# Dummy products among the first weight folds, one key-value step later, nine fill products less, and w_in loaded by halves of its rows

## The chip, the cores and the metric

The kernel runs on one core of a Trainium2 chip. The metric is the device time of one execution in microseconds; three runs of the kernel before took 252.22, 252.37 and 252.92 us, the median is 252.37. Five engines work side by side, each on its own list of instructions in order: TensorE (PE, with the loading of its weights as PEld), VectorE (DVE), ScalarE (ACT), GpSimd (POOL) and SyncE (SP), which issues DMAs. Semaphores order them among each other.

## The reference

A block of two parts over one sequence of 2048 rows of 448 columns. `mod` gives a shift, a scale and a gate for each part from a vector `c`.

```
mod = silu(c) @ w_mod                       # sa, ca, ga, sb, cb, gb: 448 each
h = layernorm(x) * (1 + ca) + sa
qkv = h @ wqkv                              # 16 heads of 28
phi_k = softmax(k w_phi), softmax(-k w_phi) # the same for q
kv, z = sum over rows of phi_k x v, of phi_k
x = x + ga * ((phi_q kv) / (phi_q z + 1e-6)) @ wo
h = layernorm(x) * (1 + cb) + sb
z = gelu(h @ w_in)                          # 1792 columns: z1 and z2
g = w_sp @ layernorm(z2) + b_sp             # w_sp is 2048 x 2048
x = x + gb * ((z1 * g) @ w_out)
```

## The kernel before

The rows are cut into 16 tiles of 128. The order of all work is written out by hand: the string `ORDER` is a list of words, each one step of the program, and every engine does its share of the steps in that order. A word such as `kM:10@B1` names the step (`kM`), its arguments (tile 10) and the PSUM bank that it writes (`@B1`); `/V`, `/S`, `/G` name the engine. There are five banks or pairs of banks, `A0` to `A2` and `B0`, `B1`, and a new tile in a bank waits until the old one is read, or, if nobody read it, until it is written.

The steps that the change and the prediction touch, with their lines:

- `du` (L725): dummy products of 128 x 256 zeros into a bank, read by nobody. 28 of them stand at the program's start.
- `ct` (L736) turns the row `c` into columns in bank `B0`; `ce:1` to `ce:4` (L743 to L749) make silu(c) of it, `f_scol`, the last step on VectorE.
- `csA`, `ccA` (L760) multiply w_mod's first two sections by `f_scol`: 16 products of one column each. `esA` puts the shift into `f_Ga` (L767), `ecA` the scale into `f_ca` (L764).
- `FTk`, `ETk`, `FSk`, `PFk`, `EPk` fold w_phi into the key weights: transposes on TensorE (L809) and copies (L813, L815), one-column products with the shift (L826), products with a block matrix (L836), and copies scaled by `f_ca` into `f_Wk` (L787 on VectorE, L783 on ScalarE). `FTq`, `ETq` and so on do it for the query. `SHv` (L774) is the shift of the value weights. `X` (L867) transposes a tile of x.
- `kM`, `vM` (L877, L885) are the key and value products of a tile, `kE`, `kF` (L880) the exponentials, `kS`, `kR`, `kP` (L891, L895, L898) the sums, their reciprocals and the normalised features `f_phik`, and `kA` (L908) the key-value step: it adds phi_k x v of one tile to `kvacc`.
- `nM` (L960) is the numerator's product, `dm` (L965) fill products of 32 zero columns into an unused part of its bank, `SHw` (L779) the shift of w_in's columns, 448 at a time, over all 448 rows in four blocks; `SCw` (L783, L785, L787) scales w_in in place. `wM` and `wN` (L996, and L994 with x added on TensorE) are the products with wo.
- `ld:win0`, `ld:win1` load w_in on ScalarE's DMA queue.

After these come the products with w_in (L1040, L1069), the large product with w_sp (L1115, L1136) and the one with w_out (L1150).

Of the kernel before, what the change touches and what calls it, by code (L numbers as in the profile page):

```python
# [15 lines left out]
P = 128  # L16
# [5 lines left out]
FH = 896  # L22
# [459 lines left out]
ORDER = """du:2@A1 ld:wk/S ld:x1/Y l1s:1 l1e:1,2/V l1r:1,2 tbl du:3@A2 ld:c/S du:3@A0 m1/G ld:x0/Y ld:wsa/Y m2a/V du:3@B1 du:14@A1 m4 ld:phi/Y du:3@B0 l1s:0 ct@B0  # L482
l1e:0,1/G l1a:1/V FTk:0@A0 ce:1 m3 ld:x2/Y X:1@A1 XE:1/V ce:2 ce:3 ce:4 ETk:0/S FTk:1@A2 ETk:1/S l1s:3 csA@B1 l1r:0,1 ld:wca/Y esA m2b/V l1a:0/G X:0@A2
bd/G FSk@A0 l1s:2 FCk/V ccA@A1 l1e:2,4/G PFk:1@B1 ecA EPk:1/V l1r:2,4 l1a:2/G XE:0/S ld:wv/Y PFk:3@A2 ld:wq/Y PFk:0@B0 EPk:0/S PFk:2@A0 ld:x5/S SHv@A1
SCv:0/S EPk:2/V EPk:3/V kM:0@B0 l1a:3/V SCv:2/V FTq:0@B1 ld:x3/Y SCv:1/S ETq:0/V kE:0 FTq:1@A1 ld:x4/Y ld:wmgb/S ETq:1/S X:2@A2 XE:2/V kF:0 kM:1@A0 l1s:4
FSq@B1 l1s:5 X:3@A1 kF:1 PFq:1@A2 l1s:6 kE:1 kM:2@B0 l1s:7 SCv:3/G FCq/S EPq:1/S XE:3/S vM:1@A0 vC:1 kS:1 vM:0@B1 ld:wo/S PFq:3@A2 kF:2 PFq:2@A0 vM:3@A1
kE:2 vM:2@B0 EPq:3/S PFq:0@A2 scb l1s:9 vC:0 ld:wmga/S vC:3 EPq:0/S kM:3@B1 EPq:2/S gr:1@A1 l1s:11 l1s:13 vC:2 qM:1@A0 kE:3 kF:3 qE:1 kS:0 l1e:4,8/G l1r:4,8
kR:0 gr:0@B1 ge:0 ge:1 qF:1 qM:0@A2 l1s:8 kR:1 qE:0 l1a:6/G l1a:4/G l1a:5/G l1s:10 T1:4,6 l1a:7/G T1:6,8 kM:4@B0 kM:5@B1 l1s:12 kP:0/G l1s:15 qF:0 kS:2
kR:2 kE:4 kS:3 l1s:14 qM:2@A1 kA:0@A0 kP:1/G kR:3 kF:4 kP:3/V kE:5 qF:2 kA:1@A0 l1e:8,12/G kP:2/V W:0,4 l1e:12,16/V kM:7@B0 kF:5 kF:7 kS:4 kE:7 kS:5 kA:2@A0
kR:5 kP:5/V l1r:8,12 l1a:8/G l1a:9/G l1a:11/G kA:3@A0 kM:6@A2 vM:5@B0 vM:4@B1 wos:0/G wos:3/V l1a:10/G T1:8,10 kR:4 kS:7 qE:2 l1r:12,16 vC:5 kP:4/V kF:6  # L490
kE:6 kS:6 kR:6 kP:6/V T1:10,12 vC:4 kM:9@A1 vM:6@B0 l1a:13/G kR:7 ld:wcb/Y ld:wsb/S l1a:14/G l1a:12/G T1:12,14 kM:8@A2 kE:9 kF:8 l1a:15/G kE:8 kP:7/G vC:6
kS:8 kA:4@A0 kM:10@B1 kR:8 kF:9 kP:8/G kS:9 kE:10 kA:5@A0 T1:14,16 vM:8@A2 kF:10 vM:9@A1 kR:9 kP:9/G vC:8 vC:9 kM:11@B0 vM:7@A2 vC:7 kS:10 kM:12@A1 kE:11
kF:11 kE:12 kR:10 kA:6@A0 kA:7@A0 kS:11 vM:10@A2 kM:14@B0 kP:10/V kF:12 kR:11 vC:10 ld:wout/Y kS:12 kF:14 vM:11@A1 vC:11 ld:win0/S kM:13@B1 vM:12@A2 kR:12
kE:14 kA:8@A0 kP:11/G W:0,0 kF:13 kM:15@B0 kS:14 kE:13 vC:12 kE:15 kA:9@A0 kS:13 kR:13 kP:12/G kF:15 ld:win1/S kS:15 kP:13/V vM:14@B1 vM:15@A2 vM:13@B0
kR:14 vC:13 kA:10@A0 kA:11@A0 kR:15 kP:14/V kA:12@A0 vC:14 kA:13@A0 kA:14@A0 kP:15/V vC:15 kA:15@A0 KV:0/V KV:1/V qM:3@A2 KZ:0 KZ:1 nM:0@A1 wos:1/V qE:3
nX:0 nM:1@A0 nX:1 qF:3 csB@B0 esB nC:1 ccB@B1 SHw:2@B0 qM:4@A2 nC:0 nS:0 nT:0 nA:0/G qM:5@A1 wos:2/G nT:1 T2:0,1 qE:4 nA:1/V qF:4 T2:1,2 W:0,1 nM:2@A0
nX:2 ecB SCw:0,2/V nC:2 nM:3@A2 nX:3 SHw:1@B1 wN:0@B0 qE:5 SCw:0,1/S nC:3 nS:1 nT:2 SHw:3@B1 nM:4@A0 nT:3 qF:5 nM:5@A1 SCw:0,3/S wN:1@B1 nX:4 wR:0/S nA:2/G
nX:5 wQ:0/S nA:3/V wR:1/S T2:2,4 wQ:1/S W:0,6 W:1,0 nC:4 nC:5 nS:2 dm:9,3 SHw:0@B0 SCw:0,0/S nT:4 qM:6@A2 qF:6 wts:6/V nT:5 nA:4/V nA:5/V nM:7@A0 nM:6@A1
wN:3@B1 nX:7 T2:4,6 SCw:1,0/G nX:6 qE:6 wN:2@B0 wR:3/S SCw:3,1/G nC:7 wR:2/S nC:6 nS:3 SCw:2,1/V nT:7 nT:6 nA:6/V qM:7@A2 W:0,3 l2R:0,2/G wQ:3/S l2r:0,2
l2a:1/G wQ:2/S qE:7 nM:9@A0 nM:8@A1 SCw:1,1/V l2a:0/G nX:8 nC:8 wN:4@B1 wM:5@B0 nX:9 nC:9 T3:0,1 qF:7 zM:0@A2 nA:7/G l2R:2,4/G SCw:3,0/V wR:4/S gt nS:4  # L500
nT:9 T2:6,8 nT:8 nM:10@A0 wM:6@B1 zG:0 nM:11@A1 T3:1,2 nX:10 nX:11 wR:5/V l2r:2,4 l2a:3/G l2a:2/G T3:2,4 wR:6/V W:1,3 wQ:4/V zM:1@A2 nC:11 nC:10 nA:9/G
SCw:2,0/S wQ:5/S wM:7@B1 zG:1 l2R:4,6/G l2r:4,6 nA:8/V T2:8,10 yM:0,0@B0 yG:0,0 W:0,7 nM:13@A2 nX:13 nS:5 zQ:0/S nT:10 wR:7/V wQ:7/S nT:11 nA:11/V zQ:1/V
zM:2@A0 zG:2 zR:0,2/V wQ:6/S zM:3@A1 nM:12@A0 wts:0/V wM:8@B0 l2a:4/G nX:12 zG:3 nC:13 l2a:5/G T3:4,6 l2R:6,8/G nA:10/V l2r:6,8 wM:9@B1 zM:4@A1 zG:4 nC:12
nS:6 nT:13 nM:15@A2 wR:8/V T2:10,12 nT:12 wQ:8/S l2a:6/G l2a:7/G wR:9/V zW:0,2 yM:0,1@B0 nM:14@A1 nX:15 T3:6,8 W:2,3 nC:15 wts:3/G zM:5@A0 nX:14 yG:0,1
wQ:9/S nC:14 nS:7 zQ:3/S yM:0,4@B1 yG:0,4 wts:1/G nA:12/V nT:14 wN:11@B0 nA:13/V wR:11/S nT:15 yM:1,3@B1 yG:1,3 wN:10@A1 zQ:2/V W:0,5 zN:1/G yM:1,1@B1
zM:6@A2 nA:14/G zN:0/G zG:5 yG:1,1 wR:10/S nA:15/V W:2,5 wQ:11/S T2:12,14 yM:0,5@B1 T2:14,16 W:2,4 zR:2,4/V yG:0,5 wM:12@B0 wQ:10/V l2R:10,12/V l2R:8,10/V
l2r:10,12 l2a:10/V zW:2,4 zQ:4/S wM:13@A0 wR:13/V yM:1,0@B1 wR:12/V wQ:12/V W:1,1 zQ:5/S zN:2/G yG:1,0 zG:6 yM:1,5@A1 l2r:8,10 wQ:13/V l2R:12,14/G yG:1,5
wts:4/V zM:7@A0 l2a:8/V zG:7 wM:14@B0 wR:14/V wM:15@B1 W:2,2 zQ:6/S l2r:12,14 W:2,7 l2a:9/G T3:8,10 zQ:7/S yM:1,4@A1 yG:1,4 wR:15/V wQ:15/S l2a:11/V yM:0,2@A2
ld:bsp/Y T3:10,12 W:1,7 l2a:12/V zR:4,6/G zR:6,8/V zW:4,6 zN:4/G yM:0,3@B1 yM:1,6@B0 l2a:13/V yG:0,2 zN:3/V yM:1,2@A0 yG:1,6 zM:9@A2 guard@A1 yG:1,2 zG:9
zN:5/V zM:8@A0 zW:6,8 zM:10@A1 zG:8 wQ:14/V l2R:14,16/G l2r:14,16 yG:0,3 yM:2,1@B0 zG:10 zN:7/G zM:11@A0 yM:2,6@A1 zN:6/V l2a:14/V T3:12,14 zQ:8/V zQ:9/S  # L510
zG:11 yG:2,6 W:1,4 zM:13@A2 zR:8,10/G zW:8,10 wts:5/V yM:2,2@A0 zM:12@A1 zQ:11/S zQ:10/V yG:2,2 zN:8/G W:2,0 yM:2,5@B1 zG:13 l2a:15/V T3:14,16 W:1,2 yM:2,4@A2
zR:10,12/G zW:10,12 yG:2,1 zG:12 W:0,2 zQ:12/S zQ:13/V yM:3,6@A0 yG:2,4 yG:3,6 zM:14@A1 yG:2,5 W:1,5 zN:9/V zM:15@A2 yM:3,3@A0 zG:14 yG:3,3 zN:11/V zN:10/V
zG:15 zQ:14/V yM:3,0@B1 zQ:15/S yM:3,1@A1 yM:3,2@A2 yG:3,2 wts:2/V yM:2,0@A0 W:2,1 yG:3,1 yM:3,5@B0 yG:3,5 yM:0,6@A2 W:1,6 sS:0,1,0,8/V sS:0,2,0,8/V yG:2,0
yM:3,4@A1 yM:2,3@A0 zR:12,14/V zR:14,16/G zW:14,16 tT:1,1/V tT:1,0/V zN:14/V zW:12,14 zN:15/V zN:13/G yG:2,3 yG:0,6 yG:3,0 zN:12/V tT:3,0/V tT:2,0/V gM:1@B0
sS:0,3,0,8/V yG:3,4 gal tT:2,1/V tT:1,2/V P:0,1,1 tT:2,2/V P:0,0,1 P:0,0,7 W:3,2 P:0,0,6 sS:0,4,0,8/V W:2,6 d:0,0,1 W:3,5 P:0,1,6 d:0,1,1 d:0,1,3 d:0,0,2
tT:3,2/V tT:4,0/G gM:0@B1 d:0,0,3 P:0,0,2 tT:4,2/G P:0,0,5 gG:1 gG:0 d:0,0,4 x:0,0,4/G P:0,1,5 d:0,0,5 W:3,4 d:0,0,7 P:0,2,1 W:3,1 P:0,0,3 P:0,0,4 d:0,0,6
d:0,1,2 x:0,0,6/V d:0,0,8 d:0,1,5 x:0,0,8/V tT:3,1/V P:0,1,2 W:3,0 d:0,1,4 P:0,2,6 P:0,1,3 x:0,0,7/V d:0,2,1 d:0,2,3 d:0,2,2 x:0,1,4/G P:0,2,7 P:1,0,1
# [740 lines left out]
```

## Time and profile before

| | |
|---|---|
| Median of three runs | 252.37 us |
| The profiled execution | 252.36 us |
| Its span, first to last instruction | 250.5 us |
| TensorE busy | 243.3 us (97%), 1517 products |
| VectorE busy | 185.4 us (74%) |
| ScalarE, GpSimd busy | 104.2 us (42%), 125.2 us (50%) |
| Mean granted TensorE clock | 0.992 |
| Chain of waits by engine | PE 77%, DVE 12%, POOL 4%, DMA 3% |

All times below count from the span's start. The chain of waits is followed back from the last instruction: at each step to what released it, or to the instruction before it on its engine. A row of the timeline gives the start, the time from there to the end of the last of a merged group, the engine, the line, the operation, out<-in and the count; in brackets stands idle time ahead of it and what ended it. Products are pipelined, so the length of one is more than the distance from one to the next. The granted clock is 1.00 at full speed.

### The profile page before, as it was taken

The page shows a single profiled execution, that of the slowest core. Times are in us where ns is not written, and L with a number is a line of the kernel's source. Part 1 is how long each engine was busy: PE and PEld are TensorE (multiplying, and loading weights), DVE is VectorE, ACT ScalarE, POOL GpSimd, SP SyncE. Part 2 cuts the span into 40 slices and gives each one's busy share as a digit, 9 for nine tenths or more (in the row PEclk, how much of TensorE's full clock was granted, in tenths as well). Part 3 has the DMA queues.
Part 4 walks back from the last instruction along what each step waited for, and adds up shares of the span by engine and source line. Part 5 has one row for each costly group of instructions (what it writes and reads, how often), then busy time and mean ns, then how long its engine had stood idle before and what let it go on. Part 6 is the DMA issues. An engine that isn't in the chain of part 4 may idle for free.

```text
span 250.5 us, 4157 instructions
## 1 busy us (share of the span) xinstructions
PE 243.3 (97%) x1517; PEld 127.0 (51%) x1517; DVE 185.4 (74%) x371; ACT 104.2 (42%) x220; POOL 125.2 (50%) x166
## 2 busy tenths in 40 slices
PE   7999999999999999999999999999999999999993
PEld 5765565666656554444444444444444444444451
DVE  5869999987799999885359799496876435644552
ACT  2488986836988966986777300000000000000000
POOL 3718996713298685586816764110119511024430
PEclk9889999999999999999999999999999999999999
DMA  7986559870587969789790981000001000101022
GB/s 176 267 245 154 104 111 257 178 190 1 94 155 139 153 125 177 131 145 219 136 171 1 179 160 41 3 0 0 0 3 38 0 0 3 55 0 37 18 79 82
DMA packets 68655, 25.22 MB, mean 101 GB/s; under 512 B 58129, under 2 KB 68498, under 8 KB 68626
## 3 DMA queue, kind: packets, MB, share of 16 engines
q1 hardware_dynamic: 64848, 20.78, 42.1%
q10 hardware_dynamic: 3778, 4.09, 6.2%
q8 instruction: 14, 0.23, 0.4%
q14 instruction: 15, 0.12, 0.2%
HBM read 8.87 MB, written 1.84 MB: 43 GB/s over the span
## 4 chain that ended last, share of the span: by engine, by line
PE 77%; DVE 12%; POOL 4%; DMA 3%; issue 1%; ACT 1%; DVEq 0%; POOLq 0%
PE g_ps L1115 29%; PE o_ps L1150 8%; PE z_ps L1069 7%; PE z_ps L1040 7%; PE g_ps L1136 6%; PE x_ps L996 3%; DVE f_ksum L891 3%; PE v_ps L885 3%; DVE f_st L843 3%; PE k_ps L877 2%; PE q_ps L932 2%; PE kvacc L908 2%; PE num L960 2%; PE warm_ps L725 2%; DMA f_hT<-f_xpad 2%; DMA f_ar<-f_ar 1%
## 5 line engine op out<-in xcount | busy, mean ns | idle before, releaser
L1124 DVE TENSOR_TENSOR f_zb<-g_ps,f_zb 128x512 f32<-128x512 f32 (+1 forms) x31 | 20.3, 668 | 18.5 <-PE g_ps L1115 18.1
L1115 PEld LDWEIGHTS <-f_z2n 128*128 128x128 bf16 x192 | 18.8, 98 | 22.5
L1131 POOL TENSOR_TENSOR f_z1T<-f_zb,f_z1T 128x512 bf16<-128x512 f32 (+1 forms) x11 | 12.0, 1102 | 35.6 <-DVE f_zb L1124 35.6
L1040 PE MATMUL z_ps<-f_ar,f_hT 112*128 112x448 bf16 (+1 forms) x128 | 26.7, 352 | 0.5 <-DMA f_hT<-f_xpad 0.5
L1069 PE MATMUL z_ps<-f_hT,f_ar 113*128 113x512 bf16 (+1 forms) x112 | 26.4, 378 | 0.1
L1150 PE MATMUL o_ps<-f_wout,f_z1T 128*128 128x448 bf16 x112 | 22.5, 352 | 0.0
L1115 PE MATMUL g_ps<-f_ar 128*128 128x512 bf16 x96 | 22.2, 379 | 0.0
L1131 POOL TENSOR_TENSOR f_z1T<-f_Sx,f_z1T 128x512 bf16<-128x512 f32 x6 | 7.3, 1221 | 26.4 <-DVE f_Sx L1124 26.4
L937 ACT ACTIVATE f_Eq<-q_ps 112x1024 bf16<-112x1024 f32 x16 | 16.2, 1037 | 6.5 <-PE q_ps L932 6.5
L1072 ACT ACTIVATE f_z1T<-z_ps 128x512 bf16<-128x512 f32 x28 | 15.9, 594 | 6.0 <-PE z_ps L1069 5.8
L1040 PEld LDWEIGHTS <-f_hT 112*128 112x128 bf16 (+1 forms) x128 | 11.9, 97 | 12.8 <-DMA f_hT<-f_xpad 2.0
L1044 ACT ACTIVATE f_zb<-z_ps 128x896 bf16<-128x896 f32 x16 | 14.6, 915 | 6.8 <-PE z_ps L1040 3.7
L980 DVE TENSOR_TENSOR f_ar<-num,f_w 128x896 bf16<-128x896 f32 x16 | 17.1, 1087 | 0.5
L1069 PEld LDWEIGHTS <-f_ar 113*128 113x128 bf16 (+1 forms) x112 | 10.8, 97 | 12.9 <-issue 0.4
L880 ACT ACTIVATE f_E<-k_ps 128x448 bf16<-128x448 f32 x32 | 16.0, 558 | 2.7 <-DVE f_phik L898 2.0
L891 DVE TENSOR_REDUCE f_ksum<-f_E 128x32 f32<-128x896 bf16 x16 | 16.6, 1051 | 0.1
L1115 PE MATMUL g_ps<-f_Eq,f_z2n 128*128 128x512 bf16 x72 | 16.7, 379 | 0.0
L1150 PEld LDWEIGHTS <-f_z1T 128*128 128x128 bf16 x112 | 10.9, 98 | 10.7
L1153 DVE TENSOR_TENSOR f_xpad<-o_ps,f_x 128x448 bf16<-128x448 f32 x16 | 9.8, 620 | 8.0 <-PE o_ps L1150 6.8
L877 PE MATMUL k_ps<-f_Wk,f_hT 113*128 113x448 bf16 (+1 forms) x64 | 15.4, 366 | 0.0
L1115 PEld LDWEIGHTS <-f_ar 128*128 128x128 bf16 x96 | 9.4, 98 | 11.2
L932 PE MATMUL q_ps<-f_hT,f_Wq 113*128 113x512 bf16 (+1 forms) x64 | 15.0, 379 | 0.0
(202 smaller groups left out, 489.2 us busy)
## 6 DMA issues: line engine op xcount, KB each, us to landing
out_dram<-f_xpad SPq DMA_DIRECT2D x16, 112.0 KB, 1.7
f_ar<-in_B_w_in_dram ACTq DMA_DIRECT2D x2, 784.0 KB, 5.8
f_wm<-in_w_mod_dram SPq DMA_DIRECT2D x3, 406.0 KB, 5.9
f_x<-in_A_x_dram SPq DMA_DIRECT2D x2, 448.0 KB, 8.8
f_wmg<-in_w_mod_dram ACTq DMA_DIRECT2D x2, 392.0 KB, 4.3
f_wout<-in_B_w_out_dram SPq DMA_DIRECT2D x1, 784.0 KB, 5.8
f_bsp<-in_B_b_sp_dram SPq DMA_DIRECT2D x1, 512.0 KB, 4.3
f_x<-in_A_x_dram ACTq DMA_DIRECT2D x1, 448.0 KB, 7.3
```

The source lines that it names most:

```text
L877: nc.tensor.matmul(t[:, 0, 0:D], lhsT=hT[0:KR[m], i, m, :], rhs=Wk[0:KR[m], m, :], start=(m == 0), stop=(m == KC - 1))
L880: nc.scalar.activation(out=Er[i % NR][:, s, :], in_=ps["k" + str(i)][:, 0, 0:D], func=ACT.Exp, scale=1.0 - 2.0 * s)
L891: nc.vector.tensor_reduce(out=ksum[:, i], in_=Er[i % NR][:].rearrange("p s (c f h) -> p (s c) h f", c=4, h=HP), axis=AX.X, op=ALU.add)
L932: nc.tensor.matmul(t[:, u, :], lhsT=Wq[0:KR[m], m, cc * CB:cc * CB + P], rhs=hT[0:KR[m], 4 * st:4 * st + 4, m, :], start=(m == 0), stop=(m ...
L937: nc.scalar.activation(out=Eq[st // 2][0:CB, 2 * c2:2 * c2 + 2, s, (st % 2) * 512:(st % 2 + 1) * 512], in_=ps["q" + str(n)][0:CB, :, :], f ...
L980: nc.vector.tensor_tensor(out=tr[i % 2][:], in0=numv(i)[:, :, :, 0:DH], in1=wr[i // 2 % 2][:, i % 2].unsqueeze(3).to_broadcast([P, 2, H, D ...
L1040: nc.tensor.matmul(t[:, hf, 0:D], lhsT=hT[0:KR[m], i, m, :], rhs=win_s[0:KR[m], m, FH + hf * D:FH + (hf + 1) * D], start=(m == 0), stop=(m ...
L1069: nc.tensor.matmul(t[:, 0, :], lhsT=win_s[0:KR[m], m, fc * P:(fc + 1) * P], rhs=hT[0:KR[m], 4 * st:4 * st + 4, m, :], start=(m == 0), stop ...
L1115: nc.tensor.matmul(g, lhsT=sta[:, m, :], rhs=mov[:, m, :], start=(m == 0 and i in (1, 6, 7)), stop=(m == 7), skip_group_check=True)
L1124: nc.vector.tensor_tensor(out=o, in0=x, in1=y, op=ALU.add)
L1131: eng.tensor_tensor(out=z, in0=T[r][:, c0:c1], in1=z, op=ALU.mult)
L1150: nc.tensor.matmul(ps["o" + str(t)][:, 0, 0:D], lhsT=later["z1T"][:, FO[n], t * P:(t + 1) * P], rhs=wout_s[:, FO[n], :], start=(n == 0), s ...
```

## The change

Four edits:

1. `ORDER` gets fourteen more dummy products: 3, 2 and 2 in bank B0 ahead of `csA`, 2 in B0 ahead of `FSk`, 2 and 1 in B0 ahead of `ccA`, and 2 in A1 ahead of the second product of the key's fold.
2. `kA:4` and `kM:10` change places: the key-value step of tile 4 is issued one product later.
3. The nine fill products `dm:9,3` ahead of `SHw:0` are left out, and so is the function.
4. w_in is loaded by halves of its 448 rows, each row whole (3584 bytes), and no more by halves of its columns (1792 bytes of every row).

The words `wM` and `wN` become one word with the engine of the step behind them; what they issue stays the same.

```diff
-... ETk:1/S l1s:3 csA@B1 l1r:0,1 ... bd/G FSk@A0 l1s:2 FCk/V ccA@A1 ... ld:wv/Y PFk:3@A2
+... ETk:1/S l1s:3 du:3@B0 du:2@B0 du:2@B0 csA@B1 l1r:0,1 ... bd/G du:2@B0 FSk@A0 l1s:2 FCk/V du:2@B0 du:1@B0 ccA@A1 ... ld:wv/Y du:2@A1 PFk:3@A2
...
-... vC:6 kS:8 kA:4@A0 kM:10@B1 kR:8
+... vC:6 kS:8 kM:10@B1 kA:4@A0 kR:8
...
-... nC:5 nS:2 dm:9,3 SHw:0@B0
+... nC:5 nS:2 SHw:0@B0
...
-        "win0": lambda q: load_rows(q, win_s[0:CB, :, 0:FH], B_w_in[:, 0:FH]),
-        "win1": lambda q: load_rows(q, win_s[0:CB, :, FH:2 * FH], B_w_in[:, FH:2 * FH]),
+        "win0": lambda q: load_rows(q, win_s[0:CB, 0:2], B_w_in[0:2 * CB]),
+        "win1": lambda q: load_rows(q, win_s[0:CB, 2:4], B_w_in[2 * CB:]),
...
-    def dm(n, i):
-        for _ in range(n):
-            nc.tensor.matmul(ps["n" + str(i)][:, 1, 480:512], lhsT=zero[:, 0:P], rhs=zero[:, 0:32], start=True, stop=True)
```

How the instructions stand now, at three places, all on TensorE. In the changed kernel the line numbers are 42 lower (46 lower behind the removed function). In brackets stands which engine (or DMA queue) the row waits for.

The first is between the last transpose of the key fold and the first one-column product with w_mod. Before, with the product of `ct` that stands further ahead, in bank B0:

```order
L736 LDWEIGHTS f_c_row [waits DMAHW5_49]
L736 MATMUL ct_ps<-f_one,f_c_row 112x1 [waits PE_49]
...
L809 MATMUL tps<-f_ident,f_wk_raw 112x112
L760 LDWEIGHTS f_wm_117 [waits DMAHW3_49]
L760 MATMUL cf_ps<-f_scol,f_wm_117 128x1 [waits DVE_49]
```

And now:

```order
L767 MATMUL tps<-f_ident,f_wk_raw 112x112
L683 LDWEIGHTS f_zero [waits DVE_49]
L683 MATMUL warm_ps<-f_zero 128x256 [waits PE_49]
...
L683 LDWEIGHTS f_zero
L683 MATMUL warm_ps<-f_zero 128x256 [waits PE_49]
...
L683 MATMUL warm_ps<-f_zero 128x256 [waits PE_49]
...
L718 LDWEIGHTS f_wm_117 [waits DMAHW3_49]
L718 MATMUL cf_ps<-f_scol,f_wm_117 128x1
```

The wait for VectorE has moved from the one-column product to the first dummy's weights, and the first product of each of the three dummy tiles waits for TensorE's own earlier work.

The second is the key-value step of tile 4. Before:

```order
L877 MATMUL k_ps<-f_Wk,f_hT 128x448
L908 LDWEIGHTS f_phik [waits DVE_49]
L908 MATMUL kvacc<-f_vaug,f_phik 128x116 [waits Activation_49]
...
L877 LDWEIGHTS f_hT [waits DMAHW4_49]
L877 MATMUL k_ps<-f_Wk,f_hT 128x448 [waits PE_49]
```

And now:

```order
L835 LDWEIGHTS f_hT [waits DMAHW4_49]
L835 MATMUL k_ps<-f_Wk,f_hT 128x448 [waits Activation_49]
...
L866 LDWEIGHTS f_phik [waits DVE_49]
L866 MATMUL kvacc<-f_vaug,f_phik 128x116
```

The key product of tile 10, with its waits for a DMA and for ScalarE, stands ahead of the step's wait for VectorE.

The third is ahead of the last shift of w_in, before:

```order
L996 MATMUL x_ps<-f_ar 128x448
L965 LDWEIGHTS f_zero
L965 MATMUL num<-f_zero 128x32 [waits DVE_49]
...
L779 LDWEIGHTS f_Gb
L779 MATMUL sh_ps<-f_ar,f_Gb 128x448 [waits Activation_49]
```

The rows of L965 are gone now, and the rows around them follow each other.

50 lines of the change are left out of this document (4 added, 46 removed).

## The prediction

> **What bounds the kernel now.** I read the page first, then the chain of waits in order of time, then the engines around the places that the change touches. TensorE is busy for 97% of the span by the page, and in the row of its granted clock (tenths, 40 slices of 6.3 us) the second and third slice are below full:
>
> ```profile
> PEclk9889999999999999999999999999999999999999
> ```
>
> In windows of 3.41 us, laid where the clock changes, the drop is one whole window at half speed, from 11.18 to 14.59. The window before it has TensorE busy for 2.98 of 3.41 us, but with 69 short products:
>
> ```profile
> 7.77:11.18 3.41, 2.98 (x69) 2.87 (x69) 3.14 (x13) 1.57 (x4) 2.33 (x6) 1.00 1.12 261
> 4.36:7.77 3.41, 3.20 (x39) 2.72 (x37) 2.66 (x13) 1.02 (x3) 2.96 (x12) 1.00 1.16 261
> 11.18:14.59 3.41, 3.41 (x15) 1.70 (x14) 1.91 (x5) 1.94 (x4) 2.38 (x4) 0.50 1.10 316
> ```
>
> (Columns: stretch, length, busy us and instructions of PE, PEld, DVE, ACT, POOL, then granted clock, DMA share, GB/s.) The chain of waits (start, us, what) goes along TensorE through these windows to the first copy of the query fold, then along VectorE for 23 us, then along TensorE, and crosses to GpSimd at 68.5:
>
> ```profile
> 8.20 0.54 PE cf_ps L760 x16
> 8.74 0.33 PE xt_ps L867 x4
> 9.07 0.88 PE fs_ps L826 x16
> 9.95 0.40 PE cf_ps L760 x16
> 10.35 0.88 PE pf_ps L836 x16
> 11.23 1.60 PE sh_ps L774 x4
> 12.83 1.49 PE k_ps L877 x4
> 14.33 0.60 PE tps L809 x8
> 14.95 0.62 DVE f_wTq L815
> ...
> 37.72 0.56 DVE f_phik L898
> 38.27 0.05 issue
> 38.32 0.59 PE kvacc L908 x8
> ...
> 67.92 0.22 PE num L965 x9
> 68.13 0.40 PE sh_ps L779 x2
> 68.63 2.24 POOL f_ar L785 x2
> ```
>
> So a shift of the query fold's copy at 14.95 is passed on by VectorE to 38.27, and what TensorE gains or loses between 38.3 and 68.5 reaches the end as well.
>
> **The dummies: what they cost.** Durations come from these rows, the first of the dummies' group (ns min/median/max, first and last start), the others of the timeline:
>
> ```profile
> L725 PE MATMUL warm_ps<-f_zero x13: 272/273/354, 4.2 to 5.6; 128*128 128x256 bf16 x13
> ...
> 5.37 0.60 PE L725 MATMUL warm_ps<-f_zero 128*128 128x256 bf16 x4
> 6.03 0.31 PE L736 MATMUL ct_ps<-f_one,f_c_row 1*112 1x1 bf16 x4
> 7.04 0.57 PE L809 MATMUL tps<-f_ident,f_wk_raw 112*112 112x112 bf16 x8
> 7.99 0.16 DVE L749 TENSOR_TENSOR f_scol<-f_e,ct_ps 112x4 bf16<-112x4 f32 x1
> 9.01 0.94 PE L826 MATMUL fs_ps<-f_Ga,f_wk_raw 112*112 112x1 bf16 x16
> 9.81 0.54 PE L760 MATMUL cf_ps<-f_scol,f_wm 112*128 112x1 bf16 x16
> 10.67 1.88 DVE L787 TENSOR_SCALAR f_Wk<-pf_ps,f_ca 112x448 bf16<-112x448 f32 x3
> 11.16 1.68 PE L774 MATMUL sh_ps<-f_wv,f_Ga 112*128 112x448 bf16 x4
> 15.39 0.93 PE L877 MATMUL k_ps<-f_Wk,f_hT 113*128 113x448 bf16 x4
> ```
>
> A dummy of 256 columns lasts 0.27 us by itself and four take 0.60, so they start (0.60 - 0.27) / 3 = 0.11 us apart. The last of these four starts at 5.37 + 3 x 0.11 = 5.70 and ends at 5.97; the next product, which uses the same bank B0, starts only at 6.03. That is 0.33 us after it instead of 0.11. In the program that product waits for TensorE itself, since the bank's writer must have finished. So each time a dummy tile follows another one in the same bank, 0.22 us are added. The fourteen come as 3+2+2 (B0), 2 (B0), 2+1 (B0) and 2 (A1): three such places. On a 448-column product the half clock shows: four take 1.68 at 11.16, and 0.93 at 15.39, so 0.37 against 0.19 us apart.
>
> The seven ahead of csA do not fill TensorE's idle 0.58 us there. Their bank B0 held the transposed c row, which VectorE reads until 8.15 (7.99 + 0.16), the same instruction that csA waits for. They start at 8.20, and csA follows after 4 x 0.11 + 2 x 0.33 + 0.11 = 1.21 us, at 9.41. cf takes 0.40 from there and xt four times 0.055 (9.81, 10.03); two dummies bring FSk to 10.25 instead of 9.01 (+1.24; it waited 0.1 before, which they fill). Three more (0.11 + 0.33 + 0.11 = 0.55) put ccA at 11.60 instead of 9.81 (+1.79), the last two put the end of the key folds' products at +2.01, and the value shift at 13.09 instead of 11.16 (it waits about 0.1 there now).
>
> At full clock the value shift and the first key product take 8 x 0.18 = 1.4 us less. But a new wait appears: the three scaled copies of the key fold take 0.63 each on VectorE. The first starts at 10.67 + 1.79 = 12.46, the second when its product is there (13.24 + 0.04), so the third ends at 14.54. The first key product's fourth part needs it and starts at 14.59 instead of 14.42. The query fold's transposes then start at 14.78, and their copy at 14.78 + 0.57 + 0.04 = 15.39 against 14.95: **+0.45 us**, although the clock stays up. Bounds: without the three extra 0.22 the same walk ends at 14.74 (**-0.2**); if the clock drops all the same, a window at half speed (8 x 0.18 and about 0.15 on the transposes, 1.6 us, as now) comes on top (**+2.0**).
>
> **Does the clock stay up?** I count what was streamed at full speed: 0.19 us for 448 columns, 0.11 for a dummy, 0.05 for 112 columns ((0.57 - 0.22) / 7 from the row at 7.04), 0.055 for 128, nothing for one column. The window that led to the drop (7.77 to 11.18) had four transposes and sixteen fold products, 1.02 us, 30%. The one before it (4.36 to 7.77) had 13 dummies and 20 transposes, 2.44 us, 72%, and no drop followed. With the change the first has 11 dummies (seven, two, and those at 11.05 and 11.16) and four transposes, 1.43 us, 42%. If transposes do not count, the bounds are 23% and 42%, and the change reaches 35%. Linear between the bounds that is a chance of 0.29 by the first count and 0.63 by the second; I go by the second, whose bounds lie closer, and keep the drop as a rival with 0.37.
>
> [...]
>
> **The key-value step.** TensorE stood idle for f_phik before kvacc of tile 4. Rows of the timeline, by engine, and the DMA view's time to landing of the transpose issued at 33.81:
>
> ```profile
> 37.24 0.73 PE L877 MATMUL k_ps<-f_Wk,f_hT 112*128 112x448 bf16 x3
> 38.32 0.59 PE L908 MATMUL kvacc<-f_vaug,f_phik 128*128 128x116 bf16 x8 [0.35 <-DVE f_phik L898]
> 36.25 0.55 ACT L888 CAST f_vaug<-v_ps 128x448 bf16<-128x448 f32 x1
> 33.81 1.23 SPq L859 DMA_TRANSPOSE f_hT<-f_xpad  x1
> ...
> 41.35 0.98 ACT L888 CAST f_vaug<-v_ps 128x448 bf16<-128x448 f32 x2
> 42.21 0.92 PE L885 MATMUL v_ps<-f_wv,f_hT 113*128 113x448 bf16 x4
> ...
> f_hT<-f_xpad SPq DMA_TRANSPOSE x1, 3.1
> ```
>
> The next product could go at 37.81 (37.24 + 3 x 0.19). kM:10, now first, has its bank free at 36.80 (the copy at 36.25) and its operand landed at about 36.9 (the transpose of 33.81, 3.1 us to landing). It takes 0.76 and then f_phik is there (38.27). So kvacc of tile 5 starts 0.51 earlier: the upper bound. VectorE and ScalarE do not move with it: v_ps at 42.21 reuses the bank that the first of the two copies at 41.35 empties at 41.9, which leaves 0.26: the lower bound. I take **-0.35**. kvacc of tile 4 itself ends 0.25 later; what overwrites its operands comes after 41 us, so nobody waits.
>
> **The nine fill products** take 0.22 (67.92 in the chain) straight ahead of the product that releases GpSimd. Between 0, should the bank of SHw:0 not be free, and 0.22; ScalarE reads that bank until 67.24, so **-0.22**:
>
> ```profile
> 66.68 0.56 ACT L1001 ACTIVATE f_x<-x_ps 128x448 bf16<-128x448 f32 x1
> ```
>
> **w_in by rows** moves nothing on the chain:
>
> ```profile
> 49.86 0.32 ACTq L643 DMA_DIRECT2D f_ar<-in_B_w_in_dram  x1
> 58.13 0.55 PE L779 MATMUL sh_ps<-f_ar,f_Gb 112*128 112x448 bf16 x2
> ...
> f_ar<-in_B_w_in_dram ACTq DMA_DIRECT2D x2, 784.0 KB, 5.8
> ```
>
> The second half is issued at 49.86 and needs 5.8 us to landing (the page's part on DMA issues, last row), 55.7. Its first reader starts at 58.13 and needed the second half before, too; now it needs both. The cover is 2.4 us; if it were gone, only a landing later than that would cost. I take 0, also for the half as many rows of twice the length.
>
> **The sum:** 0.45 - 0.35 - 0.22 = -0.12. The profiled execution took 252.36 (span 250.5 and 1.86 around it), the median of the runs is 252.37. Forecast **252.2**, no change.
>
> **The rivals.** (1) *The clock falls all the same* (slower, 0.37). One mechanism: the dummies stream too little in some window between 6 and 13 us, so TensorE runs a window at half speed as now, and pays for fourteen products besides. The copy comes at +2.0, the sum is 2.0 - 0.35 - 0.22 = +1.4: **253.8**. It decides from the point where the needed share lies above 35 to 42%. For it: FSk still streams nothing for 0.9 us, and one profile does not tell where the windows start in another execution. Against it: by the second count 42% kept the clock in the window at 4.36, and 35% is nearer to that than to 23%. (2) *The self-waits cost nothing* (faster, 0.23): the wait at 6.03 belongs to that product's own operand of one row, not to the bank. Then the copy comes 0.2 earlier, and with the key-value step at 0.45: -0.2 - 0.45 - 0.22 = -0.87, **251.5**. Against it speaks that TensorE's start at 6.03 follows the end at 5.97 as closely as other semaphore waits do (38.27 to 38.32). (3) That the dummies do nothing because they fill idle time only is excluded by the start of the seven, at the end of the same wait.
>
> **How the numbers follow.** Forecast 0.40, clock falls 0.37, self-waits free 0.23. The forecast's own range, by the bounds (+0.55 to 0 for the dummies, 0.26 to 0.51, 0 to 0.22) is 251.7 to 252.7. The range to both rivals: 251.4 to 254.0. A measurement here tells 0.3% (0.76 us) from no change: below 251.6 lies most of rival 2 and a little of the forecast (0.24), above 253.1 most of rival 1 and a little of the forecast (0.36), between them 0.40.
>
> **What would show it.** Granted clock 1.00 in all windows from 5 to 18 us; csA 1.2 us after f_scol; gaps of 0.33 at three dummies; three f_Wk copies with a gap after the first; the copy f_wTq near 15.4; no wait of kvacc for f_phik at 38 us. A window at 0.50 shows rival 1, gaps of 0.11 throughout rival 2. A later stretch that lengthens (after 70 us), or a drop that falls on other products, would make the sum wrong.

## The result: 1.4% slower, with the clock up, and the profile after

The changed kernel takes 255.26 us (median of 6 runs, 254.96 to 257.74), the kernel before beside it 252.3: a ratio of 1.0138, 95% interval 1.0092 to 1.0184. The forecast was 252.2 in a range to 254.0. A second measurement, on another chip, gave 1.0115 (1.0076 to 1.0154). The ratios leave out executions that took over 1.5% longer than the fastest of the same kernel.

The page of the changed kernel, profiled in an execution of 255.15 us (span 253.3; code lines are 42 lower than in the kernel before, 46 lower behind the removed `dm`). First the granted clock and the chain's shares by engine, then who TensorE waited for (us in total, times, longest):

```profile
PEclk9999999999999999999999999999999999999999
PE 68%; DVE 11%; DMA 7%; POOL 6%; issue 3%; SPq 3%; ACT 2%; DVEq 0%; POOLq 0%
```
```profile
PE warm_ps L683 <- DVE f_zero L641: 1.2, 1, 1.2
PE g_ps L1090 <- DVE f_z2n L1017: 1.2, 1, 1.2
PE num L918 <- DVE f_ar L934: 0.9, 1, 0.9
PE warm_ps L683 <- DVE f_scol L707: 0.6, 1, 0.6
PE k_ps L835 <- ACT f_vaug L846: 0.6, 1, 0.6
```

The window at half speed is gone, as forecast. But three waits stand there that the kernel before did not have: of g_ps for the normalised z2, of num for VectorE, and of a key product. The chain of waits leaves TensorE at each of them (start, us, what):

```profile
20.76 5.20 DMA f_wmg<-in_w_mod_dram
25.96 0.05 issue
26.01 0.93 PE gr_ps L901 x4
...
42.80 0.78 PE v_ps L843 x4
43.58 0.02 issue
43.60 0.55 ACT f_vaug L846
44.14 0.93 PE k_ps L835 x4
```
```profile
69.78 0.13 DVE f_ar L934
69.91 0.88 issue
70.78 0.15 DVE f_wout L907
70.94 0.81 issue
71.75 1.09 DVE f_ar L934
72.84 0.05 issue
72.88 0.61 PE num L918 x8
...
128.56 1.31 SPq L1031
129.87 0.04 issue
129.91 5.53 DMA f_Eq<-in_B_w_sp_dram
...
142.17 1.90 DVE f_z2n L1017 x3
144.07 0.05 issue
144.12 1.04 PE g_ps L1090 x4
```

Where the time went is seen by matching TensorE's products one by one between two traces. The table gives by how many us the same product starts later than in the profile of before, at the times that it has there; the last column is the difference of the spans. (Worked out from the traces; the other kernels are those of the experiments.)

```
at (us, before)      6.0   18.1   30.4   42.6   46.7   67.0   73.0   87.5  128.7   span
changed            +0.10  +0.69  +0.96  +0.43  +1.18  +1.18  +1.83  +1.72  +1.74   +2.8
after_again        +0.26  +0.78  +0.78  +0.52  +1.19  +1.20  +1.85  +1.52  +1.54   +3.3
half_wide_again    +0.74  +1.64  +1.64  +1.38  +1.38  +1.38  +2.04  +2.04  +1.62   +1.6
dummies_only       +0.86  +2.73  +2.73  +3.04  +3.04  +3.04  +3.03  +4.40  +3.91   +5.0
count_only         +0.98  -0.67  -0.21  -0.36  -0.35  -0.36  -0.12  +1.28  +0.92   +1.9
no_dummies         +1.10  +2.69  +2.68  +2.74  +2.74  +2.74  +3.39  +3.21  +2.88   +3.0
swap_only          +1.14  +2.65  +3.04  +2.70  +2.70  +2.70  +2.69  +2.89  +3.05   +3.0
no_fill_only       -0.13  -0.26  +0.20  +0.08  +0.08  +0.08  +0.85  +0.51  +0.42   +0.7
rows_only          +1.01  -0.63  -0.63  -0.32  -0.32  -0.32  -0.33  +0.28  -0.27   +0.1
three_free_changed +0.81  -0.59  -0.56  -0.54  -0.54  -0.54  +0.12  -0.22  -0.66   -0.2
```

In the changed kernel the front costs 0.69, the swap gives 0.5 at 39 us and loses 0.75 at 44, the missing fill products give 0.23 at 69 and lose 0.88 at 72, and 1.27 more are lost at 141. The first column is when the c row's first product starts: it varies by over a us between executions of the same front (-0.13 in no_fill_only, +1.14 in swap_only). So an execution's lag at 18 us is no measure of an edit unless that start and the clock are looked at, and the spans of swap_only and no_dummies, whose profiled executions had two windows at half speed, are no measure of these kernels' times; their ratios below are.

### The profile page after: what moved, and what is told of

Its sections match the earlier page's. It is cut to its first block, busy times and chain, and to the rows that moved or that the text cites. A ratio compares the mean times of both kernels' runs of the same rounds, so it can differ in the third digit from the quotient of the medians.

```text
span 253.3 us, 4156 instructions
## 1 busy us (share of the span) xinstructions
PE 243.2 (96%) x1512; PEld 127.4 (50%) x1522; DVE 186.9 (74%) x371; ACT 104.5 (41%) x220; POOL 127.5 (50%) x166
## 4 chain that ended last, share of the span: by engine, by line
PE 68%; DVE 11%; DMA 7%; POOL 6%; issue 3%; SPq 3%; ACT 2%; DVEq 0%; POOLq 0%
PE g_ps L1069 28%; PE o_ps L1104 8%; PE k_ps L835 5%; PE g_ps L1090 4%; PE v_ps L843 4%; PE q_ps L890 3%; PE warm_ps L683 3%; DMA f_hT<-f_xpad 3%; PE kvacc L866 3%; PE z_ps L994 2%; DMA f_Eq<-in_B_w_sp_dram 2%; DVE f_ar L934 2%; SPq L1031 2%; DMA f_wmg<-in_w_mod_dram 2%; DVE f_ar L1054 2%
## 5 line engine op out<-in xcount | busy, mean ns | idle before, releaser
L835 PE MATMUL k_ps<-f_Wk,f_hT 113*128 113x448 bf16 (+1 forms) x64 | 14.6, 352 | 0.6 <-ACT f_vaug L846 0.6
```

What stands on the lines that cost most here:

```text
L835: nc.tensor.matmul(t[:, 0, 0:D], lhsT=hT[0:KR[m], i, m, :], rhs=Wk[0:KR[m], m, :], start=(m == 0), stop=(m == KC - 1))
```

## Experiments

**1. Each edit by itself.** Four kernels, each the kernel before with one part of the change.

```diff
 dummies_only:  l1s:3 +du:3@B0 +du:2@B0 +du:2@B0 csA@B1 ... bd/G +du:2@B0 FSk@A0 l1s:2 FCk/V +du:2@B0 +du:1@B0 ccA@A1 ... ld:wv/Y +du:2@A1 PFk:3@A2
 swap_only:     kS:8 -kA:4@A0 kM:10@B1 +kA:4@A0 kR:8
 no_fill_only:  nS:2 -dm:9,3 SHw:0@B0
 rows_only:     -win_s[0:CB, :, 0:FH], B_w_in[:, 0:FH]   +win_s[0:CB, 0:2], B_w_in[0:2 * CB]   (and the second half)
```

> The kernel before with the fourteen dummies alone; swap, fill products and w_in as before. Theory L (each edit moves the end by its own price, the sum on record): granted clock 1.00 from 5 to 18 us, TensorE +0.45 to +0.69 late from 16 us and the same to the end, 252.8 to 253.1. Theory S (an edit is paid or lost again where its shift meets later transfers and the work that VectorE and GpSimd share): +0.7 to 25 us, then other amounts at the load of the gate weights (26 us), at the transposes (43 and 142 us); 253.0 to 255.3. If it gives the whole +2.96 us of the changed kernel, the dummies are the one cause.

> The kernel before with the one product issued ahead of the key-value step. Theory L: TensorE 0.5 us earlier from 39.5, 0.26 to 0.51 of it kept to the end, 251.9 to 252.1. Theory S, for this edit: the gain is kept to 43 us because here the transpose of tile 12 is not late, but whether it reaches the end depends on later waits; 251.5 to 253. If the wait for the 13th key product (44 us in the changed kernel) shows up here too, the swap makes it and not the delay of the transposes.

> The kernel before without the nine fill products. Theory L: TensorE 0.22 us earlier from 68.1 to the end, 252.15. Theory S: GpSimd's scaling of the two w_in tiles starts 0.2 us earlier against VectorE, which then has to wait for it between 69 and 72 us as in the changed kernel (a gap of about 0.9 us ahead of the second half of num), so TensorE is 0.6 to 0.7 us late from 73; 252.9 to 253.2.

> The kernel before with w_in loaded by halves of its rows. Both theories: the first reader waits for nothing new, TensorE within 0.1 us of before all the way, 252.4; S leaves room for another landing time of the transposes that run beside these loads (50 to 57 us), which would show as a shift there.

Measured against the kernel before, with 95% intervals: dummies_only 1.0129 (1.0061 to 1.0198), swap_only 1.0001 (0.9973 to 1.0028), no_fill_only 1.0014 (0.9987 to 1.0042), rows_only 1.0003 (0.9973 to 1.0034). The dummies alone make the slowdown; of the other three none is told from nothing.

The profiles say more. The rows of the granted clock of dummies_only, then of rows_only, then of swap_only:

```profile
PEclk9979999999999999999999999999999999999999
```
```profile
PEclk9999999999999999999999999999999999999998
```
```profile
PEclk9769999999999999999999999999999999999999
```

With the dummies a window fell to half speed (12.95 to 16.36), without them none did in rows_only, and two in swap_only (10.11 to 16.93), whose front is that of the kernel before. So the drop that I read off the one profile of before does not come with the kernel: the same front had none, one and two such windows in different executions, and the dummies only move the chance (by the granted clocks at the end of this section 37 of 99 executions of the kernel before have no such window, and 12 of 17 of the changed kernel). In no_fill_only the wait of num for VectorE is there, as theory S said:

```profile
PE num L960 <- DVE f_ar L980: 0.9, 1, 0.9
```

TensorE is 0.08 us late at 67 and 0.85 at 73 there, but 0.42 at 129: part of it is taken up by slack later on. Theory L is out for the dummies and for the fill products; for the swap and for w_in nothing speaks against it.

**2. The dummies out, and the higher count of instructions without dummies at the front.** dummies_only had two waits late in the program that its front does not explain: 1.5 us for a transpose at 86 us, and about 1.0 in two pieces ahead of g_ps. Both go back to transfers that end late. Beside the transposes' queue, part 3 of the page has a queue of instruction fetches, 14 packets of 16 KB each:

```profile
q8 instruction: 14, 0.23, 0.4%
```

They come, from the third to the twelfth in the trace of before, every 241 to 272 recorded TensorE instructions, so I took them for TensorE's; the trace does not name the engine that they serve. Fourteen dummies are 28 instructions, and by this reading move the fetch against the transfers by that much. Theory F says that a fetch that falls on the tail of a transpose delays it.

```diff
 no_dummies (the changed kernel):  -du:3@B0 -du:2@B0 -du:2@B0 csA@B1 ... and the other seven
 count_only (the kernel before):   nS:2 -dm:9,3 +dm:23,3 SHw:0@B0
 wide_front (the changed kernel), the 28 dummies at the start as 14 of 512 columns (`dv`: as `du`, with `0:512` for `0:256`):
                -du:2@A1 -du:3@A2 -du:3@A0 -du:3@B1 -du:14@A1 -du:3@B0
                +dv:1@A1 +dv:2@A2 +dv:1@A0 +dv:2@B1 +dv:7@A1 +dv:1@B0
 free_bank (the kernel before):    the wide start, and l1s:3 +du:7@B1 csA@B1 ... bd/G +du:2@B0 FSk@A0 l1s:2 FCk/V +du:3@A1 ccA@A1 ... +du:2@A1 PFk:3@A2
```

> The changed kernel without its fourteen dummies: the product issued ahead of the key-value step, no fill products, w_in by rows. If the dummies are the one cause (theory D), the time is what the three single edits gave together, 252.3 to 253.0, with the wait of num for VectorE at 72 us still there and none of 1.2 us for f_z2n at 141 us. If the slowdown comes from the parts together, it stays above 254.

> The kernel before with the fill products at 68 us raised from nine to twenty-three: as many more TensorE instructions as the fourteen dummies bring (a weight load and a product each), 0.3 us of streaming, and nothing at the front. Theory F (the 16 KB instruction fetch, which comes at a fixed count of TensorE instructions, falls on the tail of the w_sp transposes and makes them land late): g_ps waits about 1.2 us for f_z2n at 141 us, 253.5 to 254.0. Theory G (the dummies act through the front alone): no such wait, 252.6 to 252.9.

> The changed kernel with the 28 dummies of 256 columns at the start made 14 of 512: the same streaming, and the count of TensorE instructions back by as much as the fourteen later dummies raise it. Theory F: the fetch comes behind the transposes' tail, the wait for f_z2n at 141 us goes, 253.8 to 254.2. Theory G: as the changed kernel, 255.0 to 255.4.

> The kernel before with fourteen dummies that wait for as little as can be: seven in B1, which is free ahead of f_scol, so that they fill TensorE's idle 0.58 us, then two, three and two, with two waits for TensorE itself in place of three (the value shift is not touched); the 28 dummies at the start wide, so that the count is that of before. By the working on record csA comes 0.5 us late in place of 1.2, the query fold's copy 0.3 to 0.4 us earlier than in before when the clock stays up. If that reaches the end: 251.8 to 252.1. If a gain at the front is taken up by later waits (as in the run with w_in by rows, 0.63 us early at 15 us and level at the end): 252.4. Theory G in the form that any dummies ahead of the folds cost 2 us and more: above 254.

Measured: no_dummies 0.9990 (0.9958 to 1.0022), count_only 1.0045 (1.0015 to 1.0076), wide_front 1.0060 (1.0022 to 1.0097), free_bank 1.0018 (0.9988 to 1.0048). Without the dummies the change is level with the kernel before, so theory D holds. And count_only, which has no dummy at the front and kept its clock (0.67 us early at 18 us), is slower: its waits of TensorE are those of dummies_only.

```profile
PE z_ps L1069 <- DMA f_hT<-f_xpad: 1.5, 1, 1.5
PE g_ps L1136 <- DVE f_z2n L1063: 0.6, 1, 0.6
PE g_ps L1136 <- POOL f_z2n L1063: 0.4, 1, 0.4
```

Fourteen more instruction pairs at 68 us, 0.3 us of work, cost 1.4 us at 79 to 87 (lag -0.12 to +1.28) and about 1.0 between 129 and the end (+0.92 to +1.9). At 86 us, too, a fetch stands beside the transpose: in count_only it starts at 82.85, nine of the transpose's sixteen completion signals come by 82.88 and the other seven at 84.59 to 84.64, while in before all sixteen came from 82.81 to 83.25 and the fetch only at 85.49. Theory G, that the dummies act through the front alone, falls. wide_front has no wait for f_z2n on VectorE, as F said, but its profile has two windows at half speed (11.28 to 18.11) and its median of 255.03 lies above F's 253.8 to 254.2, so by the median it was not decided (the executions sorted by clock, at the end of this section, decide it). free_bank kept the clock and still gained nothing: 253.79 us, above every figure expected for a gain.

How the fetch stands to the last of the four w_sp transposes that end at 132 to 137 us, in all profiles; times in us from that transpose's issue, then what VectorE waited for it. The count is of TensorE's loads and products ahead of that place, against the kernel before. (From the trace's packets.)

```
kernel               count  fetch starts  last packet  VectorE waited
wide_only              -28        10.75         3.22        0.52
no_fill_only           -18         6.04         3.38        0.40
no_dummies             -18         5.91         3.46        0.57
wide_front             -18         5.91         3.45        0.69
three_free_changed     -12         5.85         3.51        0.85
three_free              -8         5.84         3.15        0.48
half_wide               -4         5.91         3.37        0.63
half_wide_again         -4         5.77         3.05        0.45
before                   0         3.33         3.23        0.26
rows_only                0         3.28         3.31        0.57
swap_only                0         3.59         3.07        none
free_bank                0         3.71         3.86        0.94
changed                +10         3.23         4.35        2.19
after_again            +10         3.33         5.29        2.56
count_only             +28         2.00         4.34        1.50
dummies_only           +28         1.72         4.17        1.51
```

Where the fetch starts behind the last packet, or with it, that packet comes 3.05 to 3.51 us after the issue; in free_bank, where it starts just ahead of that, 3.86; in the four profiles with a higher count (three kernels) 4.17 to 5.29. The changed kernel is on the edge of it: nearly all packets were through at 133.43, 3.52 us after the issue; the fetch began at 133.14 and took 1.13 us, and the last two packets, of 4 bytes each, went at 134.25, when it ended. Of the sixteen completion signals of this transpose fifteen came at 133.74 to 133.90 and one at 135.45. In the other three the last packet went 1.1 to 1.3 us after the fetch had ended. The kernel before is on the same edge, with 0.1 us to spare. What held the late packets is not shown: the trace does not name the DMA engine of a fetch or of a packet. The collision, below, is this meeting in time of a fetch and a transpose's last packets.

The rows of VectorE where that shows, in the changed kernel, then before, then count_only (in brackets its idle time ahead, and for what):

```profile
135.67 2.29 DVE L1054 TENSOR_TENSOR f_ar<-f_Eq 128x4096 bf16<-128x4096 bf16 x1 [2.19 <-DMA f_Eq<-in_B_w_sp_dram]
```
```profile
132.00 2.29 DVE L1100 TENSOR_TENSOR f_ar<-f_Eq 128x4096 bf16<-128x4096 bf16 x1 [0.26 <-DMA f_Eq<-in_B_w_sp_dram]
```
```profile
134.16 2.29 DVE L1100 TENSOR_TENSOR f_ar<-f_Eq 128x4096 bf16<-128x4096 bf16 x1 [1.50 <-DMA f_Eq<-in_B_w_sp_dram]
```

Behind this sum of the w_sp tiles VectorE still has the last normalisations to do, and g_ps needs them: that is how a late landing at 135.5 becomes a wait of TensorE at 144.

**3. A lower count, and fewer dummies.** half_wide lowers the count of the changed kernel with as little as possible; wide_only is the control for wide dummies; the other two try to keep the clock with dummies that cost nothing.

```diff
 half_wide (the changed kernel):           -du:14@A1 +dv:7@A1
 wide_only (the kernel before):            the 28 dummies at the start as 14 wide ones
 three_free (the kernel before):           l1s:3 +du:3@B1 csA@B1, and -du:14@A1 +dv:7@A1
 three_free_changed (the changed kernel):  the fourteen dummies out, l1s:3 +du:3@B1 csA@B1
```

> The changed kernel with its fourteen dummies of 256 columns at the start made seven of 512 (the last fourteen in bank A1 ahead of the c row), all else as changed: seven weight loads and seven products less ahead of everything, so the count of TensorE instructions at 131 us is four products below that of before in place of five above. Theory F (the instruction fetch falls on the tail of the w_sp transposes): the fetch starts behind the tail, DVE no longer waits 2.2 us for the transpose and g_ps no longer 1.2 us for f_z2n, 253.8 to 254.2 where the clock stays up. Theory G (the dummies' own cost and the shift they make): as the changed kernel, 255.0 to 255.4.

> The kernel before with only the 28 dummies at its start made 14 of 512 columns. Control of the runs with wide dummies: by theory F the fetch comes later still, where no transpose is under way, 252.4 to 252.9 as before. Slower than 253.2 would say that the wide dummies cost something themselves (the clock, or the c row's products), and that the two wide runs cannot be read as a matter of count.

> The kernel before with three dummies in the free bank B1 ahead of csA, where TensorE waits 0.58 us for f_scol (they last 3 x 0.11 and 0.16 more, so csA is not moved), and the fourteen dummies ahead of the c row made seven of 512. By the count of columns over the windows seen so far (no drop after 41% and more with the transposes, a drop after 38% and less, one of each at 41%), the window at 7.8 goes from 34 to 43%, so the clock stays up, and the query fold's copy comes up to 1.6 us earlier at the price of nothing. If a gain at the front reaches the end: 251.0 to 251.8. If later waits for transfers take it up, as in the run with w_in by rows: 252.2 to 252.6.

> The changed kernel with three dummies in the free bank B1 ahead of csA in place of its fourteen; swap, no fill products and w_in by rows as changed. Against the changed kernel without any dummies (0.999 of before): the same three dummies and the same two outcomes, 250.8 to 251.6 if the clock's 1.6 us reach the end, 252.0 to 252.4 if not.

Measured: half_wide 1.0056 (1.0028 to 1.0085), wide_only 1.0006 (0.9971 to 1.0042), three_free 0.9980 (0.9954 to 1.0006), three_free_changed 0.9993 (0.9964 to 1.0021). The control is not sharp: by its ratio wide_only is level with the kernel before, but its median of 253.64 (before 252.78) lies above the 253.2 that was set as the sign that wide dummies cost something themselves. Such a cost would make the runs with wide dummies slower, so it can't be what makes half_wide faster than the changed kernel. Neither version with three dummies beats the kernel before. In three_free the window from 8.15 held 29% and the clock fell (11.56 to 14.97); in three_free_changed it stayed up, TensorE was 0.54 to 0.59 us early up to 67 us, and the span came out 0.2 shorter, 252.11 us. In this profile the gain of half a us at the front is taken up on the way, in part by the wait of num at 72 (0.66), in part in front of later transposes. Which of these waits would have to go first for it to arrive was not tried.

**4. The changed kernel beside its version with a lower count.** The two had run on different chips, and the wait at 141 us rested on one profile of the changed kernel.

> The changed kernel as it is, beside the next one on the same chip, and a second profile of it. Theory F expects the wait of g_ps for f_z2n of 1 us and more at 141 us to be there again, with the fetch ahead of the last packets of the transposes; 1.010 to 1.014 of before. If the wait was an accident of the first profile, it is gone, and the time must have another cause.

> The changed kernel with seven dummies of 512 columns in place of fourteen of 256 at its start, a second time, on the same chip as the changed kernel. Theory F: 0.8 to 1.3 us faster than the run beside it, 1.004 to 1.009 of before. Theory G (the dummies' own price alone): the two within 0.3 us of each other.

Measured: after_again 1.0115 (1.0076 to 1.0154), median 255.78; half_wide_again 1.0042 (1.0000 to 1.0083), median 254.23. Of about 2.9 us, some 1.6 to 1.8 go with the higher count, where the collision is: the difference of the medians is 1.55, that of the ratios 0.0073 x 252.7 = 1.8. The second profile of the changed kernel has all three waits again, at the same places, and names the transpose at the key product, which the first profile had put down to ScalarE:

```profile
PE g_ps L1090 <- DVE f_z2n L1017: 1.6, 1, 1.6
...
PE num L918 <- DVE f_ar L934: 0.9, 1, 0.9
...
PE k_ps L835 <- DMA f_hT<-f_xpad: 0.5, 1, 0.5
```

half_wide_again has one of the three left:

```profile
PE num L923 <- DVE f_ar L939: 0.9, 1, 0.9
```

The key product's wait is gone with the count too. In the changed kernel a fetch starts at 41.55 (at 41.35 in after_again), while the transpose of tiles 12 and 13, issued at 38.35, is under way, and it lands at 44.05, 5.7 us after its issue in place of 4.2; in before the fetch came at 42.25, and in half_wide_again at 43.57, both behind that transpose's last packets (41.37 and 43.18). In the changed kernel thirty of its thirty-two 4-byte packets were through at 42.01 and the last two only at 43.45, 0.8 us after the fetch had ended; what held them that long is not shown.

**The executions sorted by their clock.** Besides the profiled one, every execution has its span and its mean granted clock on record. In the sixteen profiles a mean of 0.996 and more goes with no window at half speed at the front, 0.989 to 0.993 with one, 0.986 and less with two. That allows kernels to be compared at an equal clock (median span in us, in brackets how many executions; only those that the ratios use):

```
                                     no window (0.995 up)   one window (0.989 to 0.994)
before                                    250.1 (37)              251.1 (58)
no_dummies, swap_only, rows_only          250.0 (11)              251.0 (17)
three_free, three_free_changed            250.3 (14)              251.0 (9)
free_bank                                 250.9 (8)               252.2 (4)
wide_only                                 251.2 (3)               251.8 (7)
half_wide, half_wide_again                252.1 (17)              254.3 (3)
wide_front                                252.3 (7)               254.1 (2)
changed, after_again                      253.6 (12)              254.9 (2)
```

Three things can be read off. A window at half speed costs the kernel before 1.0 us at the end, and 37 of 99 executions have none at all. The fourteen dummies cost 2.0 us at the end where the collision is away (252.1 against 250.1); three_free has the same seven wide dummies as half_wide and is at 250.3, so those are not the reason. And the higher count costs another 1.5 (253.6 against 252.1); wide_front, at 252.3, belongs to the versions with a lower count, as theory F said.

## Why the prediction was wrong, step by step

**The step that failed is "the sum": that beyond 70 us the front's shift and the three gains reach the end unchanged.** The prediction costed each edit at its own place and looked for what waits there. It named "a later stretch that lengthens (after 70 us)" as what would make the sum wrong, but gave it no price. It left out what 28 more instructions do to a transfer that ends 120 us later, and every stretch between was argued from dependencies only. The runs put 1.5 to 1.8 us there. The other term that failed is the clock inside the 0.45: that is a price of 2.0 less 1.6 for a removed window. The price arrived whole (2.0 at an equal clock), the window was worth 1.0 at the end, and only in those executions that have one.

**The dummies' own price: right, a little low.** Predicted starts against measured: csA 9.41 and 9.48, FSk 10.25 and 10.33, ccA 11.60 and 11.68; the first dummy, behind a c row that came 0.10 late, is itself 0.08 late (8.28). The gap of 0.33 behind a dummy tile in the same bank is there (8.51 to 8.84, 8.94 to 9.27, 11.24 to 11.57), so the rival with free self-waits (251.5) is out. The copy f_wTq was put at 15.39 and came at 15.64 (+0.69 in place of +0.45). The fold's last products ended at 13.47 in place of 13.24, so the second f_Wk copy started at 13.51 in place of 13.28, and the wait behind the third handed the 0.25 on to the query fold's transposes (15.03 in place of 14.78). VectorE's scaling of w_v now falls right ahead of the copy and takes 0.64, where it took 0.33; it ends at 15.65, but the transposes end at 15.60 as well, so it adds next to nothing:

```profile
13.51 1.28 DVE L745 TENSOR_SCALAR f_Wk<-pf_ps,f_ca 112x448 bf16<-112x448 f32 x2 [0.30 <-PE pf_ps L794]
14.71 0.39 DVE L812 TENSOR_SCALAR f_xpad<-f_x,f_nm,f_rs 128x448 bf16<-128x448 bf16 x1
15.01 0.64 DVE L745 TENSOR_SCALAR f_wv<-f_wv,f_ca 112x448 bf16<-112x448 bf16 x1
15.64 0.62 DVE L773 COPY f_wTq<-tps 112x896 bf16<-112x896 bf16 x1
```

The new wait behind three f_Wk copies came as forecast.

**The clock: right in the outcome, wrong in the reason.** It stayed up in both profiles of the changed kernel. But I went by the count without the transposes, and only the count with them puts the windows of the runs in order. The share of a window that columns fill (448 columns as 0.19 us), with and without transposes, in the window ahead of a possible drop (35% and 28% for before, where the prediction had 30% and 23%: it missed the first value-shift product, which starts at 11.16):

```
                                         with   without   clock then
three_free          from  8.15            29%      23%     falls
before, no_fill     from  7.77, 7.50      35%      28%     falls
swap, no_dummies, wide_only  from  6.6    35%     6-7%     falls
half_wide           from  9.56            37%      31%     falls
dummies_only        from  9.53            38%      32%     falls
wide_front          from  7.87            42%      35%     falls
changed, half_wide_again  from 7.97, 9.29 42%      35%     stays
rows, count_only    from  6.42, 6.37      43%      10%     stays
after_again         from  8.30            45%      39%     stays
three_free_changed  from  6.01            54%      26%     stays
free_bank           from  7.13            57%      22%     stays
```

Without transposes there is no order in it: 10% kept the clock and 35% lost it. With them the clock fell after 38% and less, stayed up after 43% and more, and did both at 42%; all other full-speed windows that start between 3.4 and 25 us in the sixteen profiles hold 48% or more, and none of them is followed by half speed. That the changed kernel's window came out at the forecast 42% and 35% owes something to luck: in after_again, where the windows lie 0.33 us later, it is 45% and 39%. Rows of the windows of rows_only (kept, then full speed) and of wide_front (lost; columns as in the prediction):

```profile
6.42:9.84 3.42, 2.74 (x48) 2.35 (x47) 1.79 (x8) 1.89 (x3) 2.86 (x8) 1.00 1.10 264
9.84:13.25 3.41, 3.41 (x59) 2.83 (x58) 3.11 (x11) 1.52 (x3) 1.84 (x5) 1.00 1.12 289
```
```profile
7.87:11.28 3.41, 2.87 (x47) 2.44 (x48) 2.21 (x9) 1.39 (x2) 1.64 (x3) 1.00 1.12 271
11.28:14.70 3.42, 3.36 (x40) 2.75 (x38) 1.25 (x6) 0.53 (x1) 1.86 (x4) 0.50 0.99 280
```

Where the windows lie against the work differs from execution to execution: in the six profiles without dummies among the folds and with the narrow ones at the start, the window ahead of a possible drop starts between 6.37 and 7.77 us (no drop in two of them, one window at half speed in two, two in swap_only and no_dummies).

Worse for the sum, the drop was priced as 1.6 us to be had, in every execution. In rows_only's profile, which kept the clock, TensorE was 0.63 us early at 18 us with a c row 1.01 late, so 1.64 better from there on, and the span was 0.1 us longer than in the profile of before. That pair understates the gain, for of the executions of rows_only without a drop it is the longest. The executions sorted by clock give 1.0 us at the end for one drop, about two thirds of its price at the front, and 37 of 99 executions of before have none. So a price of 2.0 us was set against a gain of 1.0 or nothing, and the collision came on top.

**The key-value step: right in size, lost again.** TensorE went from +0.96 to +0.43 at 39.5 us, 0.53 gained, at the upper bound of the recorded 0.26 to 0.51; of it 0.26 stays up to 67 us in half_wide_again (+1.64 to +1.38), which is the recorded lower bound, 0.34 in swap_only, nothing in no_dummies. In the changed kernel the 13th key product took it back at 44.14. The prediction checked the bank of v_ps and the operand of kM:10, not the operand of the products behind it.

**The nine fill products: right for 0.23, wrong behind it.** From 67 to 69 us the lag went down by 0.23. Then GpSimd started earlier by as much, and that turned a tie round. VectorE before and after, then GpSimd before and after:

```profile
69.61 0.38 DVE L949 TENSOR_TENSOR f_wout<-f_wout,f_ar 128x448 bf16<-128x448 bf16 x1
```
```profile
70.78 1.04 DVE L907 TENSOR_TENSOR f_wout<-f_wout,f_ar 128x448 bf16<-128x448 bf16 x1
```
```profile
68.63 2.24 POOL L785 TENSOR_SCALAR f_ar<-f_ar,f_cb 112x896 bf16<-112x896 bf16 x2 [1.60 <-PE sh_ps L779]
```
```profile
69.58 2.01 POOL L743 TENSOR_SCALAR f_ar<-f_ar,f_cb 112x896 bf16<-112x896 bf16 x2 [1.38 <-PE sh_ps L737]
```

Before, VectorE's gating of a w_out row started at 69.61 and GpSimd's second scaling at 69.62, and VectorE's took 0.38 while GpSimd's second one took 1.25. Now GpSimd's second one starts at 70.58, ahead of VectorE's at 70.78, and VectorE's takes 1.04 and ends 0.24 behind it. All eight profiles without the fill products have this wait of 0.9 us, none of the eight with them. In each kernel the one of the two that starts second takes longer (GpSimd's 1.25 where its first takes 1.01, VectorE's 1.04 in place of 0.38); why it does is not shown. The wait's price at the end is small: no_fill_only is 1.0014, not told from 1.

**w_in by rows: right, nothing.**

**What the chances had.** The forecast 0.40, rival 1 (253.8) 0.37, rival 2 0.23: the time lies above all three, and above the range. Rival 1 had the right sign by the wrong mechanism.

## What to carry to other kernels

A stretch that one profile shows at half clock is one draw: look at the same front in several executions before paying for a cure (here 37 of 99 had no drop), and ask how much of an earlier front arrives at the end (here 1.0 of 1.6 us). The mean granted clock of each execution, set beside its span, answers both without a further profile. Instructions added for no work had a second price here beside their time: the instruction fetches came elsewhere against later transfers (1.72 us after the w_sp transpose's issue in dummies_only, 3.33 in before), and an edit at 8 us was paid at 141 us (1.27 us); a version with the same work and another count (wider products) tells this price from the other. Where two engines start within some hundredths of a us of each other (69.61 and 69.62 here), an earlier start of one is no gain until the other's row has been read (VectorE's took 1.04 us in place of 0.38).

## What the runs showed of the hardware

- In the profiles of before and of the changed kernel a 16 KB instruction fetch took 0.9 to 1.6 us. In the four profiles with a higher count, where it started 1.1 to 2.5 us ahead of the last packet of the last of four w_sp transposes, that packet came 4.17 to 5.29 us after the issue; where it started behind that packet, or with it, the packet came after 3.05 to 3.51 us.
- Of the full-speed windows of 3.41 us that start between 3.4 and 25 us in the sixteen profiles, those that columns filled to 38% and less, transposes included, were followed by half speed, those filled to 43% and more were not, and 42% went both ways. Busy time did not tell them apart (2.74 of 3.42 us in rows_only kept the clock, 3.25 of 3.42 in dummies_only lost it). With one window at half speed at the front the kernel before was 1.0 us longer at the end (251.1 against 250.1).
- VectorE's gating of a w_out row took 0.38 us in before, and 1.04 in the changed kernel, where it started 0.2 us behind an instruction of GpSimd's (70.78 and 70.58).
